# A filter fold with three VectorE operations per chunk in place of six, in a kernel whose order and PSUM banks are written out as tables

## The chip, the core and the metric

The kernel runs on one core of one Trainium2 chip. A core has TensorE (PE: matmuls into PSUM), VectorE (DVE), ScalarE (ACT: activations), GpSimd (POOL) and SyncE (SP, which here only issues DMAs). They run their own instruction streams side by side and wait for each other by semaphores. The metric is the device time of one launch in microseconds (us), lower is better. Before the change the median of three runs was 221.62 us (221.31 to 222.36).

## The reference

All inputs are bf16. S = 2048 rows (tokens), D = 640 channels, F = 1536. Two branches of one input x = A_q are mixed by a gate of each row:

```python
g = sigmoid((x * gate_w).sum(-1))
# branch A: a long causal convolution of every channel with a filter of 2048 taps
k_shift = short causal convolution of k with 4 taps
kv = k_shift * v
y = irfft(rfft(pad(kv)) * rfft(pad(ssm_k)))[:2048]
a = q * (y + kv * ssm_D)
# branch B
h = gelu(layernorm(x) @ w1)            # 640 -> 640
hs = (four groups of 160 channels shifted by 1, -1, 2, -2 rows) @ w2
x1 = x + hs
b = x1 + gelu(layernorm(x1) @ w3) @ w4 # 640 -> 1536 -> 640
out = g * a + (1 - g) * b
```

The term `kv * ssm_D` is the same as adding `ssm_D` to the filter's first tap, and that is how the kernel does it.

## The kernel before, in words

Everything lives in one SBUF tensor (`arena`) and one PSUM tensor of eight banks (`PSall`), so the profile names hardly any other tile. The Python code records some 1170 operations with what they read and write. Nothing decides at run time: a table `SEQUENCE` lists the recorded operations by number, each engine and each DMA queue executes its own operations in the order of that table, and a table `PLACES` gives every PSUM tile its bank. Semaphore waits follow from reads and writes. A string `ON` picks, for some small copies and adds, one of two engines or a DMA at each place where `turn` is called.

Branch A works on five chunks of 128 channels, with channels on partitions. Time is cut into four blocks of 512 steps. For each chunk `c`:

- `h_load(c)` loads the filter, 128x2048. `h_fold(c)` prepares the even and odd halves of a real DFT: in every block of 512 it adds (e = 0) and subtracts (e = 1) each entry and its mirror entry, and puts the result, 128 x (2, 4, 256), in `fo`. Entries 0 and 128 of the blocks have mirrors of their own and are written apart. SP then transposes `fo` by DMA.
- `h_even` and `h_chunk` turn that into the filter's spectrum `HF` by matmuls with constant cosine and sine tables; ACT evicts.
- `k_load`, `v_load`, `kv`, `kv2`, `x_fwd` and `combine` do the same for kv and leave `XF`. `kv` is seven wide DVE operations and some ACT ones.
- `unit(c)` multiplies the spectra block by block, with three real products for each complex one: some twenty wide DVE operations (128x1024 to 128x3072). Five of its adds, in all chunks together, are made by POOL as an accumulating DMA from `TT` onto `ACC`, which a later DVE operation of the same chunk reads.
- `final` brings the product back to time by matmuls, turns the mirrored half with a flip matrix, multiplies by g * q and adds to the output.

Branch B is `ln1`, `mm1`, `mm2`, `ln2`, `mm3`, `mm4` over 16 tiles of 128 rows. In `mm1` the fifth group of output columns goes by a small tile `hx` that is copied in four pieces of 32 partitions to shifted places in `hT`. Each copy is a DVE operation or an SP DMA, as `ON` says. The store of branch B's first 384 columns is made in two steps: `base(t)` stores by SP, and at the end of `mm4(t)` POOL adds to it with an accumulating DMA. POOL issues these, the five accumulates of `unit` and the accumulating stores of `final` from one queue, in order.

At the start, before data has landed, PE runs 15 matmuls on a constant (`warm`), ACT runs one Gelu on a constant (`gelu`), and small parameters come in by four DMAs issued by ACT. `taps` and `dcol` transpose them by matmuls (5 columns each) and ACT copies the result to SBUF; `ssm_D` and `gate_w` come out of `dcol` in one copy (`dgT`).

Instructions are recorded by helpers, so the profile shows the helper's line: L660 every DVE `tensor_tensor`, L665 most `tensor_scalar`, L670 every ACT activation, L692 most matmuls, L237 every plain DMA, L946 the copies of `hx`, L861 and L862 the LayerNorm statistics.

Of the kernel before, what the change touches and what calls it, by code (L numbers as in the profile page):

```python
# [407 lines left out]
def _folded_dft():  # L408
# [22 lines left out]
            np.where(first, np.sin(np.pi * kodd / 2), -np.sin(w * 2 * kodd * p))]  # L431
    alt, one = (-1.) ** p, p == 0
    even[0][:, 0:1], even[1][:, 0:1] = (alt - 1) / 2, 0
    even[2][:, 0:1], even[3][:, 0:1] = one, (alt + 1) / 2
    odd = [np.cos(w * bo * p), -np.cos(w * bo * n1), -np.sin(w * bo * n0), -np.sin(w * bo * n1)]
    Rh = np.concatenate(even + odd, 1)
# [10 lines left out]
def bass_gated_mix__ssm_conv_h3__mixer_s_mlp__prompt_kernel(  # L447
# [34 lines left out]
    def ps(n, cls):  # L482
# [3 lines left out]
    SEQUENCE = [1, 4, 5, 6, 26, 7, 3, 45, 24, 8, 0, 49, 50, 51, 55, 48, 68, 9, 10, 11, 12, 13, 14, 15, 16, 69, 17,  # L486
# [68 lines left out]

    HW = S + 4
    oXF = alloc(20480)
    oHF = alloc(20480)
    oB = alloc(15360)
    oHT = alloc(DC * HW)  # L560
    oXS = alloc(NT * 640)
# [607 lines left out]
```

## Time and profile before

| | |
|---|---|
| median of three runs | 221.62 us (221.31 to 222.36) |
| the profiled execution's own time | 222.27 us |
| its span, first to last instruction | 220.2 us |
| granted TensorE clock | 0.986 of full |
| PE busy | 209.0 us (95%) |
| DVE busy | 212.1 us (96%), 418 instructions |
| ACT busy | 196.5 us (89%) |
| POOL busy | 45.7 us (21%) |
| chain that ended last | DVE 57%, PE 28%, DMA 5%, ACT 5% |

A row of groups names line, engine, operation, shapes and count, then busy time and the mean of one in ns, then the idle time of the engine just before them and what ended it. A row of a timeline gives start, length, engine, line, operation and count. Two DVE instructions that follow each other overlap by some 0.08 us, so a mean duration is longer than the distance to the next start. Rows of the DMA view give the median time from issue to landing.

### The profile page before, as it was taken

To read this page: it belongs to the slowest core of one execution; us is meant where nothing else is said; L and a number is where in the kernel's file an instruction comes from. 1 tells how busy PE (TensorE), PEld (TensorE's weight loads), DVE (VectorE), ACT (ScalarE), POOL (GpSimd) and SP (SyncE) were. 2 spreads that over 40 slices of the span, in tenths; PEclk is the share of its full clock that TensorE was granted. 3 is DMA by queue.
4 is the path that set the end of the run, shared out by engine and by line. 5 is a ranking of instruction groups with operands and counts; after the bars stand their busy time and mean duration, and the time that the engine had idled before them with its cause. 6 is when DMAs were issued, how large, how long until landed. Compare 5 with 4: busy or idle time off the path is not lost.

```text
span 220.2 us, 3837 instructions
## 1 busy us (share of the span) xinstructions
PE 209.0 (95%) x1401; PEld 125.7 (57%) x1410; DVE 212.1 (96%) x418; ACT 196.5 (89%) x326; POOL 45.7 (21%) x48
## 2 busy tenths in 40 slices
PE   6899999999999999999999999999999999999961
PEld 2598755554664446665446565456665445776730
DVE  5999999999999999999999999999999998999993
ACT  2499999999999999999999999999798978558981
POOL 1331102400010001001380103331101060645440
PEclk9999999999999999999999999999999999999995
DMA  6999998999979995898486893793198299366696
GB/s 170 346 233 214 246 207 231 177 236 193 284 246 204 383 198 95 162 174 185 120 147 110 201 193 43 163 174 71 19 160 182 65 219 246 39 74 71 74 179 119
DMA packets 79440, 37.73 MB, mean 171 GB/s; under 512 B 59001, under 2 KB 76990, under 8 KB 79422
## 3 DMA queue, kind: packets, MB, share of 16 engines
q1 hardware_dynamic: 73920, 31.91, 63.3%
q0 software_dynamic: 5328, 5.51, 18.9%
q8 instruction: 11, 0.18, 0.3%
q10 hardware_dynamic: 174, 0.07, 0.2%
q14 instruction: 7, 0.06, 0.1%
HBM read 14.88 MB, written 5.77 MB: 94 GB/s over the span
## 4 chain that ended last, share of the span: by engine, by line
DVE 57%; PE 28%; DMA 5%; ACT 5%; issue 3%; SPq 0%
DVE arena L660 46%; PE PSall L692 28%; ACT arena L670 5%; DVE arena L665 4%; DMA arena<-arena 3%; DVE arena L861 3%; DVE arena L980 2%; DMA arena<-in_A_q_dram 2%; DVE arena L946 1%; DVE arena L862 0%; DVE arena L866 0%; SPq L237 0%; DVE arena L735 0%; DVE arena L704 0%
## 5 line engine op out<-in xcount | busy, mean ns | idle before, releaser
L692 PE MATMUL PSall<-arena 128*128 128x512 bf16 (+5 forms) x1340 | 201.7, 309 | 3.4 <-ACT arena L670 1.3
L660 DVE TENSOR_TENSOR arena<-arena 128x1024 bf16<-128x1024 bf16 (+14 forms) x270 | 175.1, 712 | 1.7 <-DMA arena<-arena 0.9
L692 PEld LDWEIGHTS PSall<-arena 128*128 128x128 bf16 x1349 | 121.6, 98 | 82.7 <-ACT arena L670 3.3
L670 ACT ACTIVATE arena<-PSall 128x512 bf16<-128x512 f32 (+7 forms) x157 | 94.1, 659 | 9.6 <-PE PSall L750 4.9
L670 ACT ACTIVATE arena<-arena 128x640 bf16<-128x640 bf16 (+5 forms) x107 | 93.5, 904 | 1.9 <-DVE arena L660 1.8
L237 POOL DMA_DIRECT2D out_dram<-arena x24 | 24.1, 1133 | 67.7 <-ACT arena L670 51.7
L869 POOL TENSOR_TENSOR arena<-arena 128x2 f32<-128x2 f32 (+2 forms) x15 | 17.3, 1157 | 58.0 <-DVE arena L866 42.3
L670 ACT ACTIVATE arena<-PSall,arena 128x640 bf16<-128x640 f32 (+2 forms) x32 | 20.5, 652 | 6.8 <-PE PSall L692 6.6
L237 POOL DMA_DIRECT2D arena<-arena x5 | 4.9, 978 | 43.2 <-DVE arena L660 43.2
L980 DVE SCALAR_TENSOR_TENSOR arena<-PSall,arena 128x640 bf16<-128x640 f32 x16 | 12.9, 816 | 0.3
L665 DVE TENSOR_SCALAR arena<-arena 128x640 bf16<-128x640 bf16 (+6 forms) x35 | 11.9, 358 | 0.1
L861 DVE BATCH_NORM_STATS2 arena<-arena 128x6 f32<-128x320 bf16 x20 | 9.0, 484 | 1.3 <-DMA arena<-in_A_q_dram 1.3
L715 PE MATMUL PSall<-arena 128*128 128x512 bf16 x15 | 5.4, 529 | 2.2 <-DVE arena L712 2.2
L670 ACT ACTIVATION_READ_ACCUMULATOR arena<-arena 128x1 f32 x28 | 5.7, 204 | 0.0
L946 DVE TENSOR_SCALAR arena<-arena 32x256 bf16<-32x256 bf16 (+1 forms) x22 | 5.3, 240 | 0.4
L715 PEld LDWEIGHTS PSall<-arena 128*128 128x128 bf16 x15 | 1.8, 128 | 5.0 <-issue 2.5
L922 PE MATMUL PSall<-arena 128*128 128x128 bf16 x40 | 3.4, 220 | 0.9 <-DVE arena L665 0.9
L922 PEld LDWEIGHTS PSall<-arena 128*128 128x128 bf16 x40 | 2.4, 97 | 1.3 <-DVE arena L665 1.3
L866 DVE SCALAR_TENSOR_TENSOR arena<-arena 128x2 f32<-128x2 f32 (+2 forms) x19 | 2.9, 155 | 0.0
L718 ACT ACT_TABLE_LOAD x1 | 1.3, 1283 | 1.3 <-PEq L1154 1.3
L862 DVE BATCH_NORM_AGGREGATE arena<-arena 128x2 f32<-128x12 f32 x10 | 1.7, 192 | 0.0
L980 DVE DVE_READ_ACCUMULATOR arena<-PSall,arena 128x1 f32 x16 | 1.3, 80 | 0.0
(19 smaller groups left out, 2.9 us busy)
## 6 DMA issues: line engine op xcount, KB each, us to landing
arena<-in_A_ssm_k_dram SPq DMA_DIRECT2D x5, 512.0 KB, 5.2
arena<-in_A_q_dram SPq DMA_DIRECT2D x6, 320.0 KB, 5.7
arena<-in_B_w_dram SPq DMA_DIRECT2D x1, 1920.0 KB, 8.4
out_dram<-arena SPq DMA_DIRECT2D x16, 96.0 KB, 3.9
arena<-arena POOLq DMA_DIRECT2D x4, 384.0 KB, 5.0
out_dram<-arena POOLq DMA_DIRECT2D x16, 96.0 KB, 3.6
arena<-in_A_q_dram SPq DMA_DIRECT2D x8, 192.0 KB, 4.1
out_dram<-arena POOLq DMA_DIRECT2D x8, 192.0 KB, 4.0
```

The lines of the kernel that those rows point to most:

```text
L237: fn = lambda e: e.dma_start(out, in_, **kw)
L660: P.op(eng, lambda e: e.tensor_tensor(o, real(a), real(b), op), [a, b], [o], dve_ns(o, [a, b], 2) if eng == "dve" else 500)
L665: P.op(eng, lambda e: e.tensor_scalar(o, real(a), s1, s2, op0=op0, **({} if op1 is None else {"op1": op1})), [a] + aps, [o], dve_ns(o, [a] ...
L670: P.op("act", lambda e: e.activation(real(o), real(a), f, bias=bias, scale=scale, **({"accum_out": accum} if accum is not None else {})), ...
L692: fns.append(lambda e, l=l, r=r, i=i: e.matmul(real(o), l, r, start=(i == 0), stop=(i == last)))
L715: P.op("pe", lambda e: e.matmul(real(pw), warm[:, 0:128], warm[:, 128:640], start=True, stop=True), [warm], [pw], 427.0 if i < 14 else 216.0)
L861: P.op("dve", lambda e, o=o, i=i: e.bn_stats(o, i), [i], [o], 400)
L866: P.op("dve", lambda e: e.scalar_tensor_tensor(o, a, x, b, op0=op0, op1=op1), [a, b] + aps, [o], n_of(o) / 0.96 + 65)
L869: P.op("pool", lambda g: g.tensor_tensor(o, a, e, ALU.pow), [a, e], [o], dur)
L922: P.op("pe", [lambda e, c=c, pb=pb, xn=xn: e.transpose(real(pb)[:, 128 * c:128 * (c + 1)], xn[:, 128 * c:128 * (c + 1)], ident) for c in r ...
L946: P.op("dve", lambda e, o=hT[q, 4, c0:c0 + n], i=hx[q, :]: e.tensor_scalar(o, i, 1.0, None, op0=ALU.mult), [hx[q, :]], [hT[q, 4, c0:c0 + n ...
L980: P.op("dve", lambda e: e.scalar_tensor_tensor(x, real(pr), 1.0, x, op0=ALU.mult, op1=ALU.add, accum_out=st[1, 0][:, t:t + 1]), [pr, x], [ ...
```

## The change

In `h_fold` each of the two folds becomes one operation over 128x(4, 2, 128) that covers the entries 1 to 128 of every half block, entry 128 with it. The last element of each run falls on entry 0 of the next block and is overwritten by the third operation. For the last block it falls one element behind the chunk, so every chunk of `HF` gets 16 elements of padding (`HS = 4096 + 16`). The third operation writes all entries 0 and adds a small table `skip`, which is zero but for `ssm_D` at the filter's first tap; the separate add of `ssm_D` to the filter goes. As the difference for entry 128 now has the other sign, one row in each of two constant DFT tables changes sign. `skip` needs a memset, and `dcol` now ends in two ACT copies in place of one.

In `ON` two places change from 0 to 1: one copy of `hx` of 32x256 and one of 32x512, which were SP DMAs, become DVE operations. A copy of `hx` is now also ordered behind the neighbouring element. `unit` is written with bounds `(o0, o1)` and a constant `LAST = 5`, under which it records the same operations as before. `SEQUENCE` and `PLACES` are new throughout.

```diff
+    even[5][0] *= -1
...
+    odd[1][0] *= -1
...
-    SEQUENCE = [1, 4, 5, 6, 26, 7, 3, 45, 24, 8, 0, 49, 50, 51, 55, 48, 68, 9, 10, 11, 12, 13, 14, 15, 16, 69, 17,
...
+    SEQUENCE = [4, 8, 0, 6, 9, 28, 29, 26, 10, 5, 47, 1, 11, 12, 13, 14, 7, 15, 2, 16, 17, 27, 40, 41, 50, 51, 52,
...
-    ON = ("0000000011111111011011111111111100010000010000101111000000000000001000010010000100000100000100000000"
+    ON = ("0000000011111111111111111111111100010000010000101111000000000000001000010010000100000100000100000000"
           "0000000000000000000000000000000")
...
-    HW = S + 4
+    HW, HS = S + 4, 4096 + 16
...
-    oHF = alloc(20480)
+    oHF = alloc(5 * HS)
...
-    dgT = bfs[:, 32:42]
-    Dcol, gwT = dgT[:, 0:5], dgT[:, 5:10]
+    skip = bfs[:, 0:40].rearrange("p (c e b) -> p c e b", c=5, e=2)
+    gwT = bfs[:, 48:53]
...
+    P.op("dve", lambda e: e.memset(skip, 0.0), [], [skip], 70)
...
-    act(dgT, pr, ACTF.Copy)
+    act(skip[:, :, 1, 0], pr[:, 0:5], ACTF.Copy)
+    act(gwT, pr[:, 5:10], ACTF.Copy)
...
     def h_fold(c):
 
         k, fo = kst[c], kfo[c]
-        tt(k[:, 0, 0:1], k[:, 0, 0:1], Dcol[:, c:c + 1], ALU.add)
         kh = k.rearrange("p b (h i) -> p b h i", h=2)
-        fh = fo.rearrange("p e b (h i) -> p e b h i", h=2)
         for e, op in ((0, ALU.add), (1, ALU.subtract)):
-            tt(fh[:, e, :, :, 1:128], kh[:, :, :, 1:128], kh[:, :, ::-1, 255:128:-1], op)
-            tt(fo[:, e, :, 128], k[:, :, 384], k[:, :, 128], op)
-        ts(fo[:, :, :, 0], kh.rearrange("p b h i -> p h b i")[:, ::-1, :, 0], 1.0, None, ALU.mult)
+            f = fo[:, e, :, 1:129]
+            tt(bass.AP(f.tensor, f.offset, [f.ap[0], [256, 4], [128, 2], [1, 128]]), kh[:, :, :, 1:129], kh[:, :, ::-1, 255:127:-1], op)
+        tt(fo[:, :, :, 0], kh.rearrange("p b h i -> p h b i")[:, ::-1, :, 0], skip[:, c], ALU.add)
...
                     P.op("dve", lambda e, o=hT[q, 4, c0:c0 + n], i=hx[q, :]: e.tensor_scalar(o, i, 1.0, None, op0=ALU.mult),
-                         [hx[q, :]], [hT[q, 4, c0:c0 + n]], n / 3.84 + 65)
+                         [hx[q, :], hT[q, 4, c0 - 1:c0]], [hT[q, 4, c0:c0 + n]], n / 3.84 + 65)
```

What the tables do to the order is seen in the instruction streams. The first place is the start of ACT's stream. Its first DMAs bring the short filter (`shift_k`), `ssm_D`, the identity (`cI`) and `gate_w`. Before:

```order
L237 DMA arena<-in_A_shift_k_dram 5x512
L718 ACT_TABLE_LOAD
L718 ACTIVATE arena<-arena 128x1
L237 DMA arena<-in_A_ssm_D_dram 5x128
L237 DMA arena<-cI 128x256
L237 DMA arena<-in_gate_w_dram 5x128
L670 ACTIVATE arena<-PSall 128x10
L670 ACTIVATE arena<-PSall 128x640 x2
```

After (128x20 is the copy of `taps`, 128x1 from `arena` the constant Gelu, the two 128x5 are the copies of `dcol`, 128x640 is the first transposed LayerNorm tile):

```order
L237 DMA arena<-in_A_ssm_D_dram 5x128
L237 DMA arena<-in_gate_w_dram 5x128
L237 DMA arena<-cI 128x256
L237 DMA arena<-in_A_shift_k_dram 5x512
L671 ACT_TABLE_LOAD
L671 ACTIVATE arena<-PSall 128x20
L720 ACT_TABLE_LOAD
L720 ACTIVATE arena<-arena 128x1
L671 ACTIVATE arena<-PSall 128x5
L671 ACTIVATE arena<-PSall 128x640
L671 ACTIVATE arena<-PSall 128x5
L671 ACTIVATE arena<-PSall 128x640
```

The copy of `taps` moved to the front, ahead of the constant Gelu, and there is a second table load between the two; the DMA of `shift_k`, on which `taps` depends, moved from first to fourth.

The second place is POOL's queue around the last of the accumulates of `unit` (128x1536; the 128x384 are the adds of branch B's output, the 128x2x384 those of `final`). Before:

```order
L237 DMA arena<-arena 128x1536
L237 DMA out_dram<-arena 128x384 x2
L237 DMA arena<-arena 128x1536
L237 DMA out_dram<-arena 128x384 x3
L237 DMA out_dram<-arena 128x2x384
```

After:

```order
L237 DMA arena<-arena 128x1536
L237 DMA out_dram<-arena 128x384 x9
L237 DMA arena<-arena 128x1536
L237 DMA out_dram<-arena 128x2x384
L237 DMA out_dram<-arena 128x384 x3
```

Between the fourth and the fifth accumulate nine adds of branch B stand where two stood.

The third place is the same accumulate on DVE: the 128x2x1024 is the last operation that it waits for, and the 128x2x512 at the end is the one that reads what it adds to. Before:

```order
L660 TENSOR_TENSOR arena<-arena 128x2x1024
L660 TENSOR_TENSOR arena<-arena 128x3x2x256
L660 TENSOR_TENSOR arena<-arena 128x384 x2
L660 TENSOR_TENSOR arena<-arena 128x2048
L660 TENSOR_TENSOR arena<-arena 128x3x2x256
L660 TENSOR_TENSOR arena<-arena 128x384
L660 TENSOR_TENSOR arena<-arena 128x4x512
L660 TENSOR_TENSOR arena<-arena 128x384
L660 TENSOR_TENSOR arena<-arena 128x2048
L660 TENSOR_TENSOR arena<-arena 128x2x512
```

After:

```order
L661 TENSOR_TENSOR arena<-arena 128x2x1024
L661 TENSOR_TENSOR arena<-arena 128x384 x2
L661 TENSOR_TENSOR arena<-arena 128x2048
L661 TENSOR_TENSOR arena<-arena 128x3x2x256 x2
L661 TENSOR_TENSOR arena<-arena 128x4x512
L661 TENSOR_TENSOR arena<-arena 128x384
L661 TENSOR_TENSOR arena<-arena 128x2048
L661 TENSOR_TENSOR arena<-arena 128x2x512
```

Nine operations stood between the two, and eight do now; the missing one is a 128x384 of `final`.

More of the change, by code (lines that the diff above doesn't have):

```diff
@@ L572, in bass_gated_mix__ssm_conv_h3__mixer_s_mlp__prompt_kernel @@
     XF = V(oXF, 20480).rearrange("p (c b r n) -> p c b r n", c=5, b=4, r=2)
-    HF = V(oHF, 20480).rearrange("p (c b r n) -> p c b r n", c=5, b=4, r=2)
+    HF = [V(oHF + HS * c, 4096).rearrange("p (b r n) -> p b r n", b=4, r=2) for c in range(5)]
     hT = V(oHT, DC * HW).rearrange("p (c s) -> p c s", c=DC)
@@ L598, in bass_gated_mix__ssm_conv_h3__mixer_s_mlp__prompt_kernel @@
     four = lambda o: V(o, 2048).rearrange("p (e b k c) -> p e b k c", e=2, b=4, k=2)
-    kst = [V(oHF + 4096 * c, 2048).rearrange("p (b n) -> p b n", b=4) for c in range(5)]
-    kfo = [V(oHF + 4096 * c + 2048, 2048).rearrange("p (e b n) -> p e b n", e=2, b=4) for c in range(5)]
+    kst = [V(oHF + HS * c, 2048).rearrange("p (b n) -> p b n", b=4) for c in range(5)]
+    kfo = [V(oHF + HS * c + 2048, 2048).rearrange("p (e b n) -> p e b n", e=2, b=4) for c in range(5)]
     KT = [V(oXF + 4096 * c, 2048) for c in range(5)]
     VT = [V(oXF + 4096 * c + 2048, 2048) for c in range(5)]
-    TD = [V(oHF + 4096 * c + 2048, 2048) for c in range(5)]
-    TA, TB = V(oB + 8192, 2048), [V(oHF + 4096 * c, 2048) for c in range(5)]
+    TD = [V(oHF + HS * c + 2048, 2048) for c in range(5)]
+    TA, TB = V(oB + 8192, 2048), [V(oHF + HS * c, 2048) for c in range(5)]
     sdT = [four(oXF + 16384 if c < 4 else oHF) for c in range(5)]
     het = [four(oXF + 18432 if c < 4 else oHF + 2048) for c in range(5)]
-    evn = [V(oHF + 16384 if c < 4 else oHF + 4096, 2048).rearrange("p (o e b c) -> p o e b c", o=2, e=2, b=4) for c in range(5)]
-    eft = [V(oHF + 18432 if c < 4 else oHF + 6144, 2048).rearrange("p (m e b c) -> p m e b c", m=2, e=2, b=4) for c in range(5)]
+    evn = [V(oHF + 4 * HS if c < 4 else oHF + HS, 2048).rearrange("p (o e b c) -> p o e b c", o=2, e=2, b=4) for c in range(5)]
+    eft = [V(oHF + 4 * HS + 2048 if c < 4 else oHF + HS + 2048, 2048).rearrange("p (m e b c) -> p m e b c", m=2, e=2, b=4) for c in range(5)]
     ACC, TT = [V(oB + 3072 * i, 3072).rearrange("p (o m n) -> p o m n", o=2, m=3) for i in range(2)]
@@ L613, in bass_gated_mix__ssm_conv_h3__mixer_s_mlp__prompt_kernel @@
     pair = lambda o, n: V(o, 2 * n).rearrange("p (t d) -> p t d", t=2)
-    qA = [pair(oHF + 8192 + 768 * k if k < 5 else oHF + 4096 + 768 * (k - 5), 384) for k in range(8)]
-    qB = [pair(oHF + 12288 + 512 * k, 256) for k in range(8)]
+    qA = [pair(oHF + 2 * HS + 768 * k if k < 5 else oHF + HS + 768 * (k - 5), 384) for k in range(8)]
+    qB = [pair(oHF + 3 * HS + 512 * k, 256) for k in range(8)]
     abA = [pair(oW2 + 768 * i, 384) for i in range(4)]
@@ L618, in bass_gated_mix__ssm_conv_h3__mixer_s_mlp__prompt_kernel @@
     abB = [pair(oB + 8192 + 512 * i, 256) for i in range(8)]
-    gyB = [pair(oHF + 16384 + 512 * i, 256) for i in range(8)]
+    gyB = [pair(oHF + 4 * HS + 512 * i, 256) for i in range(8)]
     sm = V32(oSm, 388)
@@ L796, in h_chunk @@
                 mm(pr[:, r, :], pairs)
-            act(HF[:, c, :, :, 128 * j:128 * (j + 1)].rearrange("p b r d -> p r b d"), pr.rearrange("p r (b c) -> p r b c", b=4), ACTF.Copy)
+            act(HF[c][:, :, :, 128 * j:128 * (j + 1)].rearrange("p b r d -> p r b d"), pr.rearrange("p r (b c) -> p r b c", b=4), ACTF.Copy)
     def k_load(c):
@@ L1013, in mm4 @@
         P.dma("pool", out[0, 128 * t:128 * (t + 1), 0:NA], X[:, t, 0:NA], accum=True)
-    ADDS = ()
+    ADDS, LAST = (), 5
     def unit(c):
-        X4, H4 = XF[:, c], HF[:, c]
+        X4, H4 = XF[:, c], HF[c]
         tt(SX, X4[:, :, 0], X4[:, :, 1], ALU.add)
@@ L1021, in unit @@
         tt(H4[:, :, 1], H4[:, :, 1], H4[:, :, 0], ALU.subtract)
-        for o0 in (2, 0):
-            for a in range(o0 + 2):
+        for o0, o1 in ((2, 4), (0, 2)) if c < LAST else ((2, 4), (1, 2), (0, 1)):
+            for a in range(o1):
                 lo = max(o0, a)
-                n, x0 = o0 + 2 - lo, lo - a
-                acc, tmp = ACC[:, lo - o0:2], TT[:, 0:n]
+                n, x0 = o1 - lo, lo - a
+                acc, tmp = ACC[:, lo - o0:o1 - o0], TT[:, 0:n]
                 to = tmp if a else acc
@@ L1037, in unit @@
                     tt(acc, acc, tmp, ALU.add)
-            Y = XF[:, c, o0:o0 + 2]
-            tt(Y[:, :, 0], ACC[:, :, 2], ACC[:, :, 1], ALU.subtract)
-            tt(Y[:, :, 1], ACC[:, :, 2], ACC[:, :, 0], ALU.add)
-            scale(Y[0:1, :, :, 0:128], ACC[0:1, :, 0:2, 0:128], 1.0, True)
+            Y, R = XF[:, c, o0:o1], ACC[:, 0:o1 - o0]
+            tt(Y[:, :, 0], R[:, :, 2], R[:, :, 1], ALU.subtract)
+            tt(Y[:, :, 1], R[:, :, 2], R[:, :, 0], ALU.add)
+            scale(Y[0:1, :, :, 0:128], R[0:1, :, 0:2, 0:128], 1.0, True)
     def final(g, o, q, k):
```

2 lines of the change are left out of this document (1 added, 1 removed), and 129 rows, old and new, of tables (PLACES, SEQUENCE).

## The prediction

> **What bounds the kernel now.** I read the page first: busy time by engine, the chain that ended last, then the waits of DVE, then a table by stretches.
>
> ```profile
> PE 209.0 (95%) x1401; PEld 125.7 (57%) x1410; DVE 212.1 (96%) x418; ACT 196.5 (89%) x326; POOL 45.7 (21%) x48
> DVE 57%; PE 28%; DMA 5%; ACT 5%; issue 3%; SPq 0%
> ```
> ```profile
> DVE arena L861 <- DMA arena<-in_A_q_dram: 1.3, 2, 0.9
> DVE arena L660 <- DMA arena<-arena: 0.9, 1, 0.9
> DVE arena L660 <- ACT arena L670: 0.2, 1, 0.2
> PE PSall L692 <- ACT arena L670: 1.3, 2, 1.2
> ```
> ```profile
> 5.50:20.00 14.50, 13.47 (x189) 10.97 (x187) 14.32 (x54) 11.10 (x36) 3.67 (x5) 1.00 1.05 271
> 126.00:154.00 28.00, 28.00 (x164) 15.87 (x163) 27.93 (x42) 27.97 (x42) 6.56 (x7) 1.00 0.71 131
> 177.00:203.00 26.00, 25.85 (x172) 16.58 (x171) 25.04 (x36) 18.75 (x36) 11.66 (x12) 1.00 0.75 128
> ```
>
> The columns of the last block after the stretch and its length are the busy time of PE, PE's weight loads, DVE, ACT and POOL. DVE is the bound by a hair: 212.1 us of 220.2, with 2.4 us of waits for data and other engines in the whole span, and it has the largest share of the chain. But in the middle (126 to 154 us) PE, DVE and ACT are all busy for 27.9 to 28.0 us of 28. So time saved on DVE alone is worth its full price only where PE and ACT have room: before 20 us, and after 154 us, where ACT falls back first. The profiled execution took 222.27 us, 0.65 above the median of 221.62. I make the sum as differences and add it to the median.
>
> **The fold and the copies: DVE work.** These are DVE's groups by shape.
>
> ```profile
> L660 DVE TENSOR_TENSOR arena<-arena 128x1024 bf16<-128x1024 bf16 x80 | 52.0, 682 | 1.0 <-DMA arena<-arena 0.9
> L980 DVE SCALAR_TENSOR_TENSOR arena<-PSall,arena 128x640 bf16<-128x640 f32 x16 | 12.9, 816 | 0.3
> L660 DVE TENSOR_TENSOR arena<-arena 128x1016 bf16<-128x1016 bf16 x10 | 6.7, 680 | 0.0
> L946 DVE TENSOR_SCALAR arena<-arena 32x256 bf16<-32x256 bf16 x15 | 3.3, 219 | 0.2
> L946 DVE TENSOR_SCALAR arena<-arena 32x512 bf16<-32x512 bf16 x7 | 2.0, 287 | 0.1
> L660 DVE TENSOR_TENSOR arena<-arena 128x4 bf16<-128x4 bf16 x10 | 1.6, 166 | 0.0
> L665 DVE TENSOR_SCALAR arena<-arena 128x8 bf16<-128x8 bf16 x5 | 0.9, 181 | 0.0
> L660 DVE TENSOR_TENSOR arena<-arena 128x1 bf16<-128x1 bf16 x5 | 0.8, 150 | 0.0
> ```
>
> A chunk's fold was two of 128x1016, two of 128x4, one of 128x8 and one of 128x1. By means that is 2.02 us. But a small one does not keep the engine for its 0.15 to 0.18 us, as the timeline's starts show:
>
> ```profile
> 14.67 0.69 DVE L660 TENSOR_TENSOR arena<-arena 128x1016 bf16<-128x1016 bf16 x1
> 15.28 0.48 DVE L861 BATCH_NORM_STATS2 arena<-arena 128x6 f32<-128x320 bf16 x1
> 17.34 0.19 DVE L665 TENSOR_SCALAR arena<-arena 128x8 bf16<-128x8 bf16 x1
> 17.42 0.21 DVE L946 TENSOR_SCALAR arena<-arena 32x256 bf16<-32x256 bf16 x1
> 18.01 0.18 DVE L660 TENSOR_TENSOR arena<-arena 128x4 bf16<-128x4 bf16 x1
> 18.09 0.49 DVE L861 BATCH_NORM_STATS2 arena<-arena 128x6 f32<-128x320 bf16 x1
> ```
>
> From 17.34 to 17.42 and from 18.01 to 18.09: a small operation costs 0.08 us of the queue. The 128x1016 costs 15.28 - 14.67 = 0.61.
> - Removed: three small operations net for each of five chunks, 15 x 0.08 = -1.2 us. Ends: nothing, where another engine holds DVE anyway, and -2.5 us if each saved its mean ((0.150 + 2 x 0.166 + 0.181 - 0.166) x 5). I take -1.2, from the starts.
> - The ten wide ones grow from 1016 to 1024 elements: 682 against 680 ns, nothing. Both forms begin at an odd element and read the mirror backwards, and the 128x1024 row is mostly of plain operands; that the two rows agree says the odd start costs nothing here. The upper end is that the new form drops to half rate: bounded by the 816 ns for 640 elements of L980, 1.31 us for 1024, +0.6 us each, +6 us. I take 0.
> - Added: one hx copy of 32x256 and one of 32x512, 0.22 + 0.29 = +0.5, and a memset in the start, at most the 0.08 of a small operation.
>
> Sum on DVE: -1.2 + 0.5 + 0.1 = **-0.6 us**.
>
> The Trainium skill, "VectorE: DVE Perf Modes", section "Mode 2×_1P — pack two bf16 into one 32-bit read", asks for a start aligned to 4 bytes, which element 1 of a bf16 row is not; by that rule old and new fold would both run at one element per cycle. The 680 ns for 1016 elements do not bear it out, and the sum by it would be unchanged, unless the new shape alone fell to that rate.
>
> **The two DMAs that go** were on SP's queue; this is the larger one, 2.7 us from issue to landing:
>
> ```profile
> arena<-arena SPq DMA_DIRECT2D x1, 32.0 KB, 2.7
> ```
>
> DVE never waited for such a one in the list above, so nothing is gained but queue time behind the transposes; I take 0 (end: -0.3, the smallest DVE wait for input data being 0.4).
>
> **The start on ACT.** The second table load and the early copy of `taps` stand where ACT was idle:
>
> ```profile
> 1.34 1.28 ACT L718 ACT_TABLE_LOAD   x1 [1.34 <-PEq L1154]
> 1.71 0.37 ACTq L237 DMA_DIRECT2D arena<-cI  x1
> 2.11 0.34 ACTq L237 DMA_DIRECT2D arena<-in_gate_w_dram  x1
> 2.64 0.21 ACT L718 ACTIVATE arena<-arena 128x1 bf16<-128x1 bf16 x1
> 7.74 0.77 ACT L670 ACTIVATE arena<-PSall 128x10 bf16<-128x10 f32 x2 [4.89 <-PE PSall L750]
> L670 ACT ACTIVATE arena<-PSall 128x10 bf16<-128x10 f32 x1 | 0.2, 180 | 4.9 <-PE PSall L750 4.9
> ```
> ```profile
> 7.50 0.20 PE L750 MATMUL PSall<-arena 5*128 5x5 bf16 x2
> 8.56 0.45 PE L922 MATMUL PSall<-arena 128*128 128x128 bf16 x5 [0.86 <-DVE arena L665]
> ```
> ```profile
> arena<-cI ACTq DMA_DIRECT2D x1, 64.0 KB, 3.6
> arena<-in_A_q_dram SPq DMA_DIRECT2D x6, 320.0 KB, 5.7
> ```
>
> ACT's 4.89 us of idle ends at 7.74. The identity lands at about 1.71 + 3.6 = 5.3. If `shift_k`, now fourth in the place of `gate_w`, is no later, the four small matmuls take 2 x 0.20 to 5.7, and then on ACT a copy of 0.2 (as the 128x10), the load 1.28, the Gelu 0.21 and a 128x5 copy of 0.2 end at 7.6: still inside the idle time. The cover is thin, 0.15 us. If `shift_k` takes the 5.7 us that is the median of the larger loads of that time, it lands at 7.8, and everything on ACT moves by 2.3 us more. PE, whose remaining warm matmuls are queued behind `taps`, moves with it, though PE waits for DVE there until 8.56. DVE meets ACT again at the hx copies, at about 14 us. Ends 0 and +2.3; a DMA of a few rows on the same queue is nearest to cI, so I take **+0.3 us**.
>
> The Trainium skill, "ScalarE: Activation LUTs", section "What ACT_TABLE_LOAD costs", gives about 1.28 us for the load and 1.38 us more for a drain at every switch. The row agrees on the 1.28, and no drain is seen in it, since the Gelu starts at 2.64, where the load ends (1.34 + 1.28); but there nothing had run on ACT before.
>
> **The fifth accumulate.** It is the one DMA of the kernel that DVE was seen to wait for after the start:
>
> ```profile
> 176.69 0.28 issue
> 176.97 6.79 DMA arena<-arena
> ```
> ```profile
> arena<-arena POOLq DMA_DIRECT2D x4, 384.0 KB, 5.0
> out_dram<-arena POOLq DMA_DIRECT2D x16, 96.0 KB, 3.6
> L660 DVE TENSOR_TENSOR arena<-arena 128x384 bf16<-128x384 bf16 x6 | 1.9, 347 | 0.0
> 177.51 3.00 POOL L237 DMA_DIRECT2D out_dram<-arena  x3
> ```
>
> From the last producer's end at 176.69 to the landing at 176.97 + 6.79 = 183.76 are 7.1 us, of which DVE filled 6.2 and waited 0.9. Its median brother took 5.0 us to land. In the new order one 128x384 fewer covers it, 0.3 us by starts (347 ns less the overlap of 0.08), so at the same landing time DVE waits 1.2. Six adds of branch B now stand directly ahead of it on POOL's queue behind one that waits for ACT; POOL issued such adds 0.5 to 1.0 us apart (three in 3.00 from 177.51), so they are through before DVE is ready, unless ACT is late, but their data can still be in flight. Ends: -0.9, the wait gone at 5.0 us of landing, and +1.3, with one more us of queue. I take **+0.3 us**.
>
> **The rest of the order and the banks.** Which new waits the tables make elsewhere no row of before shows. Below, there is little to win: 0.2 us of waiting for ACT on DVE. Above, the nearest row is PE's longest wait for ACT, 1.2 us; with ACT's one more copy of 0.2 us that makes an end of +1.4. I take 0, with ends -0.2 and +1.4.
>
> **Sum.** -0.6 + 0.3 + 0.3 + 0 = 0.0, so 221.6 us by the median (222.3 against the profiled execution).
>
> **The rivals.**
> - *Faster.* The accumulate lands in time (-0.9 in place of +0.3) and the start stays hidden (0 in place of +0.3): 221.6 - 1.5 = 220.1. For it: the median landing of 5.0 us. Against: 6.8 us were seen at this place. The skill's "VectorE: DVE Perf Modes", section "The DRAIN you can't avoid", says that the next operation waits until the pipe is empty, so each removed operation would save its whole duration; worked out from the rows above that is -2.5 in place of -1.2, and 220.3. The starts 0.08 apart speak against it.
> - *Slower, at the start of ACT.* The second table load costs a drain as well, or `shift_k` is late. It decides from the point where the copy of `taps` begins more than 1.3 us after 5.7 us. Priced by the skill's 1.38 us of drain, ACT is free at 9.0 and the time is 221.6 - 0.3 + 1.2 = 222.5; priced by rows alone, with `shift_k` at 7.8, it is 221.6 - 0.3 + 2.3 = 223.6.
> - *Slower, by the accumulate and other waits.* The accumulate at its upper end (+1.0 over mine) and one wait of the new order at its end of 1.4: 224.0 for both, 222.6 for the first and 223.0 for the second alone. It decides where the accumulate lands over 2 us after DVE is ready for it.
> - *The fold does not get cheaper.* At half rate, 221.6 + 6 = 227.6. The row of the 128x1016 speaks against it.
>
> **How the numbers follow.** I give 0.45 to my forecast (its own range 220.6 to 222.7, which is also within 0.5%, about what a measurement of this kernel can tell from no change), 0.20 to faster (0.16 by the accumulate, 0.04 by whole durations saved), 0.14 to slower by the start, 0.19 to slower by accumulate and order, and 0.02 to the half rate: 0.20, 0.45, 0.35. The range reaches from 220.0, just under the faster case, to 223.9, between the two ends of the slower ones; about 0.05 is left below and 0.12 above.
>
> **What the profile after would show.** 128x1024 on DVE 90 times at 0.68 us and no 128x1016 or 128x4; DVE busy down by about 0.6 us. Two table loads, ACT's first tile evicted by about 7.8 us: later than 8.5 and the start was mis-sized. DVE waiting some 1.2 us for an accumulate near 182 us. PE and ACT waits in the middle no longer than before. I am wrong if DVE shows waits of more than 1 us at other places, or if the wide fold takes over 1 us.

## The result and the profile after

The changed kernel takes 220.28 us (median of 7 runs, 220.03 to 220.77) against 222.02 us (221.11 to 222.40, 7 runs) of the kernel before on the same chip: the ratio is 0.9935, with a 95% interval of 0.9919 to 0.9951. That is 1.4 us less (1.1 to 1.8), 0.65%. Differences in us are taken from the ratios, here and below, and not from the two medians, which lie 1.7 us apart here. A few launches well above the rest, of experiments 7 and 12 and of the kernel before, are in none of the ratios. My number was 221.6, with a range of 220.0 to 223.9. The time lies in the range, but it is the number of the faster rival (220.1) and not that of the likeliest case. The profiled execution took 220.28 us, with a span of 218.5 us.

First the page of the changed kernel, busy time by engine and the chain:

```profile
PE 208.4 (95%) x1400; PEld 126.0 (58%) x1410; DVE 211.1 (97%) x406; ACT 198.1 (91%) x328; POOL 44.5 (20%) x48
PE 62%; DVE 20%; DMA 8%; ACT 5%; issue 2%; SPq 1%; POOL 1%; ACTq 0%
```

DVE has 1.0 us less work (212.1 before) in 12 instructions fewer. The chain now goes mostly through PE, where it went through DVE before (57% DVE, 28% PE). Two engines that are both busy for 95% and more can change places in it without either having become slower; experiments 9 and 10 show that its largest share is not to be read as the bound.

DVE's groups by shape:

```profile
L661 DVE TENSOR_TENSOR arena<-arena 128x1024 bf16<-128x1024 bf16 x90 | 58.5, 680 | 0.2 <-DMA arena<-arena 0.2
L947 DVE TENSOR_SCALAR arena<-arena 32x256 bf16<-32x256 bf16 x16 | 3.5, 219 | 0.4
L947 DVE TENSOR_SCALAR arena<-arena 32x512 bf16<-32x512 bf16 x8 | 2.3, 286 | 0.1
L661 DVE TENSOR_TENSOR arena<-arena 128x8 bf16<-128x8 bf16 x5 | 0.9, 188 | 0.0
```

The ten wide operations of the fold have joined the 80 others of 1024 elements, and the mean went from 682 to 680 ns: their odd start costs nothing. The 128x8 addition (188 ns) stands for the 128x8 copy (181 ns), the 128x4 and the 128x1.

DVE's waits, and the same three stretches as in the prediction:

```profile
DVE arena L862 <- DMA arena<-in_A_q_dram: 0.7, 1, 0.7
DVE arena L661 <- ACT arena L671: 0.6, 2, 0.4
DVE arena L737 <- DMA arena<-in_B_w_dram: 0.5, 1, 0.5
DVE arena L661 <- DMA arena<-arena: 0.2, 1, 0.2
```
```profile
5.50:20.00 14.50, 13.77 (x190) 11.62 (x190) 13.72 (x51) 12.88 (x38) 3.71 (x6) 1.00 1.10 287
126.00:154.00 28.00, 27.95 (x162) 15.81 (x162) 28.00 (x39) 27.57 (x41) 5.53 (x5) 1.00 0.62 129
177.00:203.00 26.00, 26.00 (x175) 16.84 (x173) 25.68 (x37) 19.86 (x37) 9.35 (x10) 1.00 0.68 116
```

The wait for the accumulate fell from 0.9 to 0.2 us, and from 177 to 203 us DVE is busy for 25.68 us where it was 25.04. The wait for ACT grew from 0.2 to 0.6.

The start on ACT, from the timeline:

```profile
5.88 0.19 ACT L671 ACTIVATE arena<-PSall 128x20 f32<-128x20 f32 x1 [2.18 <-PE PSall L752]
6.08 1.28 ACT L720 ACT_TABLE_LOAD   x1
7.37 0.20 ACT L720 ACTIVATE arena<-arena 128x1 bf16<-128x1 bf16 x1
7.48 0.16 ACT L671 ACTIVATE arena<-PSall 128x5 bf16<-128x5 f32 x1
7.83 1.37 ACT L671 ACTIVATE arena<-PSall 128x640 bf16<-128x640 bf16 x3 [0.19 <-PE PSall L923]
```

The second table load ends at 7.36, the Gelu starts at 7.37, and the first 128x640 tile is evicted at 7.83, with 0.19 us of idle time ahead of it that waits for PE. The load is hidden, by as little as the prediction said.

### The profile page after: what moved, and what is told of

Read it like the earlier page. It is cut to its first block, busy times and chain, and to the rows that moved or that the text cites. A ratio compares the mean times of both kernels' runs of the same rounds, so it can differ in the third digit from the quotient of the medians.

```text
span 218.5 us, 3829 instructions
## 1 busy us (share of the span) xinstructions
PE 208.4 (95%) x1400; PEld 126.0 (58%) x1410; DVE 211.1 (97%) x406; ACT 198.1 (91%) x328; POOL 44.5 (20%) x48
## 4 chain that ended last, share of the span: by engine, by line
PE 62%; DVE 20%; DMA 8%; ACT 5%; issue 2%; SPq 1%; POOL 1%; ACTq 0%
PE PSall L693 62%; DVE arena L661 16%; ACT arena L671 5%; DMA arena<-arena 3%; DMA out_dram<-arena 3%; DMA arena<-in_B_w_dram 3%; DVE arena L981 1%; DVE arena L666 1%; SPq L237 1%; POOL out_dram L237 1%; DVE arena L947 1%; DVE arena L862 1%; PE PSall L923 0%; DVE arena L863 0%; DVE arena L867 0%
## 5 line engine op out<-in xcount | busy, mean ns | idle before, releaser
L661 DVE TENSOR_TENSOR arena<-arena 128x1024 bf16<-128x1024 bf16 (+10 forms) x260 | 173.9, 732 | 1.4 <-ACT arena L671 0.6
L671 ACT ACTIVATE arena<-PSall 128x512 bf16<-128x512 f32 (+8 forms) x158 | 94.8, 660 | 7.3 <-PE PSall L693 3.9
L671 ACT ACTIVATE arena<-arena 128x640 bf16<-128x640 bf16 (+6 forms) x107 | 93.9, 911 | 0.8 <-DVE arena L661 0.7
L870 POOL TENSOR_TENSOR arena<-arena 128x2 f32<-128x2 f32 (+2 forms) x15 | 16.1, 1079 | 68.9 <-DVE arena L867 53.7
L666 DVE TENSOR_SCALAR arena<-arena 128x640 bf16<-128x640 bf16 (+5 forms) x30 | 11.1, 393 | 0.2
L717 PE MATMUL PSall<-arena 128*128 128x512 bf16 x15 | 6.0, 549 | 2.0 <-DVE arena L714 2.0
L947 DVE TENSOR_SCALAR arena<-arena 32x256 bf16<-32x256 bf16 (+1 forms) x24 | 5.8, 241 | 0.5
```

The costliest lines, as they stand in the source:

```text
L661: P.op(eng, lambda e: e.tensor_tensor(o, real(a), real(b), op), [a, b], [o], dve_ns(o, [a, b], 2) if eng == "dve" else 500)
L666: P.op(eng, lambda e: e.tensor_scalar(o, real(a), s1, s2, op0=op0, **({} if op1 is None else {"op1": op1})), [a] + aps, [o], dve_ns(o, [a] ...
L671: P.op("act", lambda e: e.activation(real(o), real(a), f, bias=bias, scale=scale, **({"accum_out": accum} if accum is not None else {})), ...
L717: P.op("pe", lambda e: e.matmul(real(pw), warm[:, 0:128], warm[:, 128:640], start=True, stop=True), [warm], [pw], 427.0 if i < 14 else 216.0)
L870: P.op("pool", lambda g: g.tensor_tensor(o, a, e, ALU.pow), [a, e], [o], dur)
L947: P.op("dve", lambda e, o=hT[q, 4, c0:c0 + n], i=hx[q, :]: e.tensor_scalar(o, i, 1.0, None, op0=ALU.mult), [hx[q, :], hT[q, 4, c0 - 1:c0]] ...
```

## Experiments

All times below are against the kernel before, which took 221.8 to 222.0 us beside them; the changed kernel stands at -1.4. The first theory (A) is that of the prediction with the result put in: DVE is the bound, a small operation costs its place in DVE's queue, and the accumulate landed sooner. Its rivals are that the order alone brought the gain (B), and that whole durations were saved (C).

**1. The new fold in the old order.** The fold, its table, the memset and the two ACT copies are those of the change; order, banks and hx copies those of before.

```diff
-        tt(k[:, 0, 0:1], k[:, 0, 0:1], Dcol[:, c:c + 1], ALU.add)
...
+            tt(bass.AP(f.tensor, f.offset, [f.ap[0], [256, 4], [128, 2], [1, 128]]), kh[:, :, :, 1:129], kh[:, :, ::-1, 255:127:-1], op)
+        tt(fo[:, :, :, 0], kh.rearrange("p b h i -> p h b i")[:, ::-1, :, 0], skip[:, c], ALU.add)
```

> The kernel before with the new fold alone (three DVE operations a chunk, the added table and its memset, two ACT copies for one); order, banks and the two DMA copies of hx stay as they were. Theory A (the removed small operations cost 0.08 us of DVE's queue each, and DVE is the bound): 15 x 0.08 - 0.08 for the memset = -1.1 us against before, DVE's wait for the fifth accumulate stays near 0.9 us. Rival B (the small operations lay beside other work, and the whole gain of 1.4 us is the order's): 0. Rival C (each removed operation saves its whole duration): -2.4 us.

Measured: 220.98 us, ratio 0.9959 (0.9945 to 0.9973): -0.9 us (-1.2 to -0.6). B and C both lie outside. DVE's wait for the accumulate stayed:

```profile
DVE arena L664 <- DMA arena<-arena: 0.6, 1, 0.6
```

**2. The old fold in the new order.** The counterpart: order, banks and the two hx copies on DVE are those of the change, the fold is the old one. Against the changed kernel:

```diff
     for e, op in ((0, ALU.add), (1, ALU.subtract)):
-            f = fo[:, e, :, 1:129]
-            tt(bass.AP(f.tensor, f.offset, [f.ap[0], [256, 4], [128, 2], [1, 128]]), kh[:, :, :, 1:129], kh[:, :, ::-1, 255:127:-1], op)
+            tt(fh[:, e, :, :, 1:128], kh[:, :, :, 1:128], kh[:, :, ::-1, 255:128:-1], op)
+            tt(fo[:, e, :, 128], k[:, :, 384], k[:, :, 128], op)
...
```

> The kernel before with the new order, banks and the two hx copies on DVE, and the old fold of six operations: the small ones stand right beside the wide ones. Theory A: +0.5 for the two copies, -0.7 for the accumulate that lands sooner, 0 for the start: -0.2 us against before. Rival B (the gain is the order's): -1.4 us. Rival C: the order costs what the fold gave beyond 1.4 us, so +1.0 us.

Measured: 221.69 us, ratio 0.9994 (0.9977 to 1.0010): -0.1 us (-0.5 to +0.2), as A said. The four corners go together: the fold brings -0.9 us in the old order and -1.3 in the new one (-1.4 less -0.1); everything else brings -0.1 with the old fold and -0.5 with the new one. So some two thirds of the gain, or more, are the fold's.

**3. The three adds behind the accumulate, in the kernel before.** In the kernel before, POOL issues three adds of branch B right behind the fifth accumulate. I moved their three numbers in the table behind that of the DVE operation that follows the accumulate's reader.

```diff
-784, 926, 791, 829, 914
+784, 791, 926, 829, 914
```

(Only the numbers moved and their neighbours are shown.)

> The kernel before with one thing moved: the three adds of branch B that POOL issued right behind the fifth accumulate (from 177.5 us) now come behind the DVE operations that read it. Theory A (the three adds' data share the DMA engines with the accumulate, and that is why it took 6.8 us from issue to landing before and 6.0 after): the accumulate lands in about 5 to 6 us, DVE's wait of 0.9 us falls under 0.2, the time by -0.7 us. Rival D (the accumulate takes its time whatever stands behind it, its landing is set by the transfers already under way): lands in 6.8 us, wait 0.9, time unchanged.

Measured: 221.81 us, ratio 1.0001 (0.9984 to 1.0017). The edit did not do what the expectation says: two of the three numbers (829 and 914) stood behind 791 already, farther back, so only 926 changed sides. POOL's queue as it ran:

```profile
177.45 0.86 POOL L237 DMA_DIRECT2D arena<-arena  x1 [7.29 <-DVE arena L663]
177.99 2.99 POOL L237 DMA_DIRECT2D out_dram<-arena  x3
```

The three adds still go out 0.5 us behind the accumulate: a place in the table only orders instructions within a queue, and these wait for nothing on DVE. So the run decides nothing between A and D. As a repeat of the kernel before it has one use: DVE waited 0.4 us for the accumulate in it, where the kernel before showed 0.9, so this wait varies by half a microsecond from one execution to the next.

**4. Three adds behind the accumulate, in the changed kernel.** Here the move changes POOL's own order: three of the six adds that stood ahead of the accumulate now stand behind it.

```diff
-901, 865, 804, 769, 984
+769, 984, 901, 865, 804
```

(769 is the accumulate; other numbers between them left out.)

> The changed kernel with three of its six adds of branch B moved from directly ahead of the fifth accumulate to directly behind it on POOL, as the kernel before had three. Theory A: the accumulate takes 6.8 us from issue to landing in place of 6.0, DVE waits about 0.9 us for it in place of 0.2, and the time is 0.7 us more than the changed kernel's, so -0.7 us against before. Rival D: landing and wait stay at 6.0 and 0.2, the time stays at -1.4 us against before.

Measured: 220.17 us, ratio 0.9938 (0.9918 to 0.9959): -1.4 us. POOL's queue, and the accumulate in the list of DMA issues (the last number is us from issue to landing):

```profile
176.12 0.87 POOL L237 DMA_DIRECT2D arena<-arena  x1 [4.99 <-DVE arena L665]
176.66 3.00 POOL L237 DMA_DIRECT2D out_dram<-arena  x3
```
```profile
arena<-arena POOLq DMA_DIRECT2D x1, 384.0 KB, 5.8
```

With the same three adds behind it as in the kernel before, the accumulate landed in 5.8 us and DVE did not wait at all. That part of A falls: three adds issued behind the accumulate on its own queue do not bring the 6.8 us back. What SP issues behind it was not changed here.

**5. The two hx copies back on SP.** Two digits of the string that chooses between engines, in the changed kernel:

```diff
-    ON = ("00000000111111111111111111111111000100...
+    ON = ("00000000111111110110111111111111000100...
```

> The changed kernel with the two hx copies put back as DMAs on SP. Theory A (DVE is the bound there, and a copy costs it its 0.22 or 0.29 us): 0.5 us less than the changed kernel, so -1.9 us against before. Rival F (the copies fill gaps of DVE in the start, or their DMAs hold something on SP): 0, so -1.4 us against before, or slower than that.

Measured: 220.43 us, ratio 0.9943 (0.9924 to 0.9962): -1.3 us (-1.7 to -0.8). A's -1.9 lies outside; the two copies do not cost their 0.5 us. DVE's busy time fell by that half microsecond, to 210.6, and its waits for ACT took it up:

```profile
DVE arena L661 <- ACT arena L671: 1.2, 3, 0.5
```

They were 0.6 us in the changed kernel. In the profile these waits stand at 42.9 and 51.7 us.

**6. One table load.** In the changed kernel the constant Gelu (25) goes ahead of the copy of `taps` (41).

```diff
-27, 40, 41, 50, 51, 52, 71, 25, 53
+27, 40, 25, 41, 50, 51, 52, 71, 53
```

> The changed kernel with the constant Gelu ahead of the copy of taps on ACT, so that ACT loads one table in the start and not two. Theory A (the second load lay in ACT's idle time ahead of its first tile): no change, -1.4 us against before; ACT's first 128x640 eviction still near 7.8 us. Rival G (the load holds the first tile): ACT's first eviction a microsecond sooner and the time 0.3 to 1.3 us less than the changed kernel's, -1.7 to -2.7 us against before.

Measured: 220.14 us, ratio 0.9929 (0.9913 to 0.9945): -1.6 us (-1.9 to -1.2), which is the changed kernel's time within both intervals. The start on ACT:

```profile
2.42 1.28 ACT L724 ACT_TABLE_LOAD   x1 [2.42 <-issue]
5.60 0.26 ACT L675 ACTIVATE arena<-PSall 128x20 f32<-128x20 f32 x2 [1.68 <-PE PSall L756]
7.54 0.79 ACT L675 ACTIVATE arena<-PSall 128x640 bf16<-128x640 bf16 x2 [1.69 <-PE PSall L927]
```

ACT now idles for 1.69 us where the load was. Its first tile comes 0.3 us sooner, as does the copy of `taps` ahead of it (5.60 against 5.88). The load had lain in idle time.

**7. Twenty more small operations.** Four a chunk in the changed kernel, into spare places:

```diff
+        for j, n in ((40, 8), (54, 8), (192, 8), (202, 6)):
+            tt(bfs[:, j:j + n], k[:, 0, 0:n], k[:, 1, 0:n], ALU.add)
```

> The changed kernel with four more small DVE additions a chunk (three of 128x8 and one of 128x6, into spare places, so that nothing waits for them), two beside each wide one of the fold: 20 more in all. It prices the small operation by itself. Theory A (0.08 us of DVE's queue each): +1.6 us over the changed kernel, +0.2 us against before. Rival B (hidden beside other work): 0, so -1.4 us against before. Rival C (whole durations of 0.17 to 0.19 us): +3.6 us over the changed kernel, +2.2 us against before.

Measured: 221.26 us, ratio 0.9978 (0.9965 to 0.9990): -0.5 us, so 0.95 us more than the changed kernel, 0.05 us for each, give or take 0.02 by the two intervals. They are not hidden, and they do not cost their durations.

**8. SP's transfers held behind the accumulate.** Experiment 4 left open why the accumulate lands sooner in the new order. In the kernel before, six SP transfers go out in the 2.6 us ahead of it:

```profile
174.37 0.88 SPq L237 DMA_DIRECT2D arena<-in_A_q_dram  x2
175.29 0.47 SPq L237 DMA_DIRECT2D out_dram<-arena  x1
175.80 1.04 SPq L237 DMA_DIRECT2D arena<-in_A_q_dram  x2
176.88 0.47 SPq L237 DMA_DIRECT2D out_dram<-arena  x1
```

The edit makes SP's third of these (number 976, the first transfer to `out`) wait for a DVE operation that ends behind the accumulate's issue:

```diff
         turning, adding = [], None
+        ops[976].preds.setdefault(987, True)
```

> The kernel before with one wait added: SP's DMA of base(15), issued 1.7 us ahead of the fifth accumulate, waits for a DVE operation that ends 0.8 us behind the accumulate's issue, so that it and the SP transfers after it (four of which stood ahead of the accumulate or beside its issue) now queue behind it. Theory E (the accumulate's landing is set by the transfers that were queued ahead of it, 0.7 MB in the old order and 0.45 MB on SP in the new one): it lands in 5.5 us or less in place of 6.3 to 6.8, DVE's wait for it of 0.4 to 0.9 us is gone, and the time falls by about 0.6 us. Rival D (the landing does not depend on SP's transfers): lands in 6.3 to 6.8 us, time unchanged. Rival H (the wait is not on the path that sets the end): the wait goes, time unchanged.

Measured: 221.54 us, ratio 0.9990 (0.9974 to 1.0007): -0.2 us (-0.6 to +0.2). POOL, SP and the accumulate in this kernel:

```profile
176.38 0.86 POOL L237 DMA_DIRECT2D arena<-arena  x1 [7.28 <-DVE arena L661]
```
```profile
177.25 0.36 SPq L237 DMA_DIRECT2D out_dram<-arena  x1
177.65 1.80 SPq L237 DMA_DIRECT2D arena<-in_A_q_dram  x2
```
```profile
arena<-arena POOLq DMA_DIRECT2D x1, 384.0 KB, 4.3
```

With nothing of SP issued from 2.2 us ahead of it to 0.9 us behind it, the accumulate lands in 4.3 us instead of 6.3 to 6.8, and DVE's wait for it is gone. So D falls: the landing does depend on the transfers of another engine's queue. The Trainium skill, "DMA: Bandwidth & Descriptors", section "Issuing engines are not separate DMA queues", says that transfers started by any engine run on the same 16 DMA engines; the 4.3 against 6.8 us agrees. The time alone does not tell E from H here, since -0.2 with its interval holds both 0 and nearly -0.6; experiment 11 looks at that in the changed kernel.

E says more, that it is the amount queued ahead that counts, and this does not show it: the edit also moved a transfer issued 0.4 us behind the accumulate. The DMA view from the accumulate's issue to its landing has what SP's kind of queue moved meanwhile (packets, MB, share); in the kernel before, in this one and in the changed one:

```profile
q1 hardware_dynamic: 1449, 0.90, 48.0%
q1 hardware_dynamic: 259, 0.16, 13.1%
q1 hardware_dynamic: 1622, 0.94, 52.1%
```

Here almost nothing moved beside the accumulate. But in the changed kernel, where it landed in 6.0 us, as much moved as in the kernel before with its 6.8.

**9 and 10. The dose, early and late.** Since the chain of the changed kernel runs through PE from 31 us on, I formed a second theory (P): DVE's work counts only before about 40 us and in the tail. The same 24 small additions go into the folds of chunks 0 to 2 in one kernel, and into those of chunks 3 and 4 in the other.

```diff
+        for j in range((8, 8, 8, 0, 0)[c]):
+            tt(V(oJ + 8 * j, 8), k[:, 0, 0:8], k[:, 1, 0:8], ALU.add)
```

The late kernel has `(0, 0, 0, 12, 12)`.

> The changed kernel with 24 more small DVE additions of 128x8 (into spare places), eight beside the wide ones of each of the folds of chunks 0, 1 and 2, which run before 60 us. Theory A (0.08 us each, DVE is the bound throughout): +1.9 us over the changed kernel, +0.5 us against before. Theory P (PE is the bound from the point near 40 us where it runs without a gap, and DVE's work counts only before that and in the tail): also +1.9 us, or +1.3 us where chunk 2 lies behind that point, so between -0.1 and +0.5 us against before.

> The changed kernel with the same 24 small additions, twelve beside the wide ones of each of the folds of chunks 3 and 4, at 85 to 88 and 133 to 137 us. Theory A (0.08 us each, DVE is the bound throughout): +1.9 us over the changed kernel, +0.5 us against before. Theory P (PE runs without a gap there and hides them): 0, so -1.4 us against before.

Measured: early 221.48 us, ratio 0.9988 (0.9971 to 1.0005); late 221.61 us, ratio 0.9992 (0.9973 to 1.0011). Both are 1.2 us above the changed kernel. P falls: 24 small operations at 85 and at 133 to 137 us cost as much as the same 24 before 60 us, though the second of these places lies in the stretch where PE of the changed kernel is busy for 27.95 us of 28 (and DVE for all 28). The two late places were not tried apart. The price is 0.05 us each again, within 0.02. DVE's busy time grows by 1.6 us in both, to 212.7, which is 0.07 for each. In the early kernel's timeline one wide operation and four small ones stand together:

```profile
15.54 0.96 DVE L667 TENSOR_TENSOR arena<-arena 128x1024 bf16<-128x1024 bf16 x5
16.43 0.48 DVE L870 BATCH_NORM_STATS2 arena<-arena 128x6 f32<-128x320 bf16 x1
```

From start to start that is 0.89 us, 0.61 of it for the wide one by the row in the prediction, so 0.07 for each small one. By duration they take much more, here by shape in the late kernel (five of the fold's own are in the row):

```profile
L667 DVE TENSOR_TENSOR arena<-arena 128x8 bf16<-128x8 bf16 x29 | 3.0, 155 | 0.0
```

24 times 155 ns would be 3.7 us. The Trainium skill, "VectorE: DVE Perf Modes", section "The DRAIN you can't avoid", in the plain form in which the prediction used it, gives that sum; 1.2 us were measured. The section goes on to say that a next operation that is not held starts earlier, and that is the case that these runs show.

**11. The accumulate held back.** In the changed kernel the fifth accumulate also waits for a later DVE addition, and its number stands behind that one's in the table:

```diff
         turning, adding = [], None
+        ops[769].preds.setdefault(722, True)
```

> The changed kernel with the fifth accumulate issued about 2.5 us later: it waits for the DVE addition that ends at 178.5 us and not only for the one that ends at 176.0. It makes DVE's wait for it large enough to be seen in the time. Theory T (the wait lies on the path that sets the end, microsecond for microsecond): the wait grows from 0.2 to about 2.5 us and the time by as much, so about +0.9 us against before. Rival H (PE or another engine has slack for it behind 183 us): the wait grows, the time by less than half of it, -0.3 us or less against before.

Measured: 222.94 us, ratio 1.0065 (1.0037 to 1.0094): +1.4 us (+0.8 to +2.1), which is 2.9 above the changed kernel. DVE's wait:

```profile
DVE arena L666 <- DMA arena<-arena: 2.5, 1, 2.5
```

The wait grew by 2.3 us and the time by 2.9 with some 0.7 of uncertainty; the profiled executions, at 222.56 and 220.28, are 2.3 apart. So it lies on the path, all of it, and H falls for the changed kernel. Experiment 8 was made in the kernel before; its gain of 0.2 us is less than the wait of 0.4 to 0.9 that went, though its interval reaches to 0.6.

This run also bears on E. SP's transfers in the 2.4 us ahead of the accumulate, which is issued at 178.76, and the landing:

```profile
176.36 0.47 SPq L237 DMA_DIRECT2D out_dram<-arena  x1
176.87 1.52 SPq L237 DMA_DIRECT2D arena<-in_A_q_dram  x3
178.44 0.47 SPq L237 DMA_DIRECT2D out_dram<-arena  x1
```
```profile
arena<-arena POOLq DMA_DIRECT2D x1, 384.0 KB, 5.7
```

Five transfers stand ahead, nearly the six of the old order, and it lands in 5.7 us, as with three. The number of transfers ahead does not explain the difference between the two orders.

**12. Eight hx copies on SP.** Had the DVE work of the start been worth its time, this would be a faster kernel:

```diff
-    ON = ("00000000111111111111111111111111000100...
+    ON = ("00000000100000000111111111111111000100...
```

> The changed kernel with all eight hx copies of the second 512 rows (32x256 each, between 21 and 40 us on DVE) as DMAs on SP. Theory P (DVE's work counts until PE runs without a gap near 40 us): up to 8 x 0.22 = 1.8 us less than the changed kernel; as the two copies that went back to SP gave 0.3 us of their 0.5 by the end of the first matmuls at 57 us and nothing that the time showed, I expect about 0.5 us, -1.9 us against before. Rival F (ACT and PE are the bound from 20 us on, or the DMAs hold back a transpose on SP's queue): no change, -1.4 us against before, or slower than the changed kernel.

Measured: the four launches that count took 225.93 to 229.00 us, ratio 1.0212 (1.0173 to 1.0250), 4.7 us slower than before. DVE's and PE's longest waits of the start, SP's queue at that time, and the chain that ended last:

```profile
31.15 0.82 DVE L981 SCALAR_TENSOR_TENSOR arena<-PSall,arena 128x640 bf16<-128x640 f32 x1 [4.48 <-PE PSall L693]
```
```profile
28.15 8.12 PE L693 MATMUL PSall<-arena 128*128 128x320 bf16 x55 [3.20 <-DMA arena<-arena]
```
```profile
23.32 2.36 SPq L237 DMA_DIRECT2D arena<-arena  x3
25.72 1.40 SPq L234 DMA_TRANSPOSE arena<-arena  x1
27.57 1.78 SPq L237 DMA_DIRECT2D arena<-arena  x3
```
```profile
24.60 3.46 DMA arena<-arena
28.06 0.09 issue
28.15 13.91 PE PSall L693 x105
```

PE stands for 3.2 us behind an SBUF-to-SBUF DMA, and DVE for 4.5 behind PE. The copies stand on SP's queue among the transposes there. What PE waited for is a copy, the third of the first three: it was issued at 24.60 and took 3.46 us to land, where the same copy on DVE takes 0.22. The transpose issued next, at 25.72, landed only at 29.2, when PE was running again.

No kernel here is faster than the changed one by more than the intervals; experiment 6 is level with it.

## Why the prediction was right and wrong

- **The fold on DVE.** Predicted -1.2 us with +0.1 for the memset, from starts 0.08 us apart; measured -0.9 (experiment 1). The mechanism held, and the size came a little under it: 0.05 us, give or take 0.02, by the three doses, 0.06 by the fifteen that were removed. The ends were far off on both sides, and the wide operations kept their rate.
- **The two hx copies on DVE.** Predicted +0.5, their full durations. This term was mis-sized: without them the changed kernel is no faster (experiment 5, -1.3 against -1.4), and DVE waits for ACT 0.6 us longer, at 43 and 52 us. So they fill time in which DVE would have stood. With the accumulate's -0.45 below, experiment 2 leaves +0.3 for them and the difference of experiment 1 to the changed kernel 0; I put them at 0 to 0.3; the intervals are as wide as that.
- **The two SP DMAs that went.** Predicted 0. No run tests it alone; experiment 5 puts them back and gains nothing.
- **The start on ACT.** Predicted +0.3 between 0 and +2.3; it is 0 (experiment 6). `shift_k` was in time: PE's waiting matmuls were done by 5.9 us, as the 128x20 row shows, and the first tile went at 7.83 against a predicted 7.8. No drain is seen behind the second load: 6.08 + 1.28 = 7.36, and the Gelu starts at 7.37, though ACT had worked just before. The Trainium skill, "ScalarE: Activation LUTs", section "What ACT_TABLE_LOAD costs", gives 1.38 us for one, on which a rival was priced; this row does not bear it out.
- **The fifth accumulate.** This is the step that failed. I took +0.3 us: the same landing time, one operation less to cover it, and six adds ahead of it as a danger. The adds were issued by 174.1 us and did not hold the accumulate back: it was issued 0.3 us behind the end of its last producer, as before. Their data were still in flight, as I had feared, four of the six landing behind its issue; but where all six had landed (experiments 2, 7 and 10) it took 5.5, 6.1 and 6.1 us, against the 6.0 here, so no harm of theirs is seen. The landing was not the same: 6.3 to 6.8 us in the three kernels with the old order around it and SP free to run, 5.5 to 6.1 in the nine with the new one and the accumulate in its place. That SP's transfers set it in part is shown (experiment 8). The orders differ in what SP issues ahead of it: in the old one six transfers in the 2.6 us before its issue, in the new one three, and a fourth 0.1 us behind its issue at 176.29:

```profile
174.89 1.50 SPq L237 DMA_DIRECT2D arena<-in_A_q_dram  x3
176.43 0.47 SPq L237 DMA_DIRECT2D out_dram<-arena  x1
```

  But experiment 11 had five ahead and landed in 5.7, and as much was moved beside the accumulate in either order. So what makes the old order's landing later stays open. DVE's wait for it was 0.9, 0.6 and 0.4 us in the old order (before, 1, 3), and 0.2, 0, 0, 0.2, 0, 0.5, 0, 0.5 and 0 in the new one (after, 2, 4, 5, 6, 7, 9, 10, 12): 0.6 against 0.2 in the mean, with a scatter of half a microsecond. As the wait counts in full (experiment 11), I put the term at -0.45 us, not +0.3. I had SP's queue in hand only for the DMAs that were removed from it, and did not look at what it carried ahead of the accumulate.
- **The rest of the order and the banks.** Predicted 0. No wait of DVE is longer than 0.7 us, and none is new but 0.4 us for ACT and 0.5 for a load in the start; the latter, 0.8 us long, is in experiment 3's kernel with the old order too.

The sum with the measured terms is -0.9 + 0 + 0 - 0.45 = -1.35 us, against -1.4 measured; with 0.3 for the copies, -1.05, just outside the interval of 1.1 to 1.8. The terms are known to 0.3 us or so each, so that the sum closes is no proof of the split. My sum was 0.0. Of the 1.35 us between them, 0.75 are the accumulate's, 0.5 the copies' and 0.3 the start's, less 0.2 for the fold and its memset, which gave a little less than I took. The rival that came is the faster one, and for the reasons it named: the accumulate lands sooner and the start stays hidden. That its 220.1 is so near is in part luck: it took -0.9 for the accumulate, twice what came, and kept the +0.5 for the copies, which did not. That the prediction gave it 0.20 came from holding the one landing seen, 6.8 us, for a property of the place. It goes with the order, which the change rewrote.

## What to carry to other kernels

Price a small operation by the distance of starts in the timeline, not by its duration, and prove the price with a dose of them at two places: which engine has the chain did not tell here whether DVE's work was hidden. Around a DMA that an engine is seen to wait for, look at what every queue issues, and not at its own alone: to move those transfers away changed its landing by 2 us and more here (experiment 8). One landing is not a property of the place, and a count of the transfers ahead did not forecast it. Moving a number in a table of orders does nothing unless a queue's own order or a dependency changes, and the timeline shows whether it did.

## What the runs showed of the hardware beyond what I expected

- An accumulating SBUF-to-SBUF DMA of 384 KB took between 4.3 and 6.8 us from issue to landing at one place in the program. The 4.3 came where SP issued nothing from 2.2 us ahead of it to 0.9 us behind it.
- Three adding DMAs of 96 KB directly behind it on the same queue did not slow it (5.8 us with them, 6.0 without, one execution each).
- 24 operations of 155 ns cost the kernel 1.2 us, early and late in the program alike: they start 0.07 us apart.
